# Long convolution and memory attention on one core: another stored order, other PSUM banks and other eviction engines for the same operations

## The chip, the cores and the metric

The kernel runs on one core of a Trainium2 chip. The core's engines work side by side, each on its own queue in order: TensorE (PE, with its weight loads shown apart as PEld), VectorE (DVE), ScalarE (ACT), GpSimd (POOL) and SyncE (SP), which here only issues DMAs. Matmul results land in PSUM, which has eight banks; DVE or ACT must copy a result out ("evict" it) before its bank can take another group of matmuls. The metric is device time in microseconds, as the median of several runs. A profile is one further execution, with a record of every instruction.

## The reference

Two branches, joined along the last axis. S = 2048 tokens, D = 640 channels.

```python
# branch A: short filter, gate, long convolution by FFT, skip, gate
k_shift = sum of 4 shifted copies of k, each times a tap per channel
kv = k_shift * v
y  = irfft(rfft(pad(kv)) * rfft(pad(ssm_k)))[:S]      # per channel
a  = q * (y + kv * ssm_D)

# branch B: 32 heads of 20, 4 segments of 512 tokens, one after another
q, k, v = x @ wq, x @ wk, x @ wv
p     = softmax(q @ k.T / sqrt(20) + causal mask)     # inside a segment
a_mem = (phi(q) @ M) / (phi(q) @ z + 1e-6)            # memory of earlier segments
o     = g * a_mem + (1 - g) * (p @ v)
M, z  = M + phi(k).T @ v, z + sum(phi(k))
b     = o @ wo
return concat([a, b], axis=-1)
```

## The kernel before

Nothing in this kernel is issued in the order in which its Python runs. A class `Recorder` takes down 1482 operations with their engines, and 471 PSUM groups. Then `Recorder.issue` (line 247) issues them in a stored order: `ORDER` (line 990) is a packed permutation of the operations, `BASE` (line 1012) a packed list with the first PSUM bank of each group. Dependencies are kept in any order: `issue` asserts that each operation comes after all that it depends on, and semaphores are placed from the final order. So the stored order sets, for each engine, the sequence of its queue; when an instruction runs follows from the queue and its waits. A third constant, `EVICT` (line 987), has one digit for each of 227 plain PSUM copies: `evict` (line 400) gives a copy to DVE where the digit is 1, to ACT where it is 0.

**Branch A** runs as `conv` (line 439) over five blocks `dp` of 128 channels. For each: the long filter is brought to time-major form in tile `kT` (`load_filter`; block 0 by four groups of PE transposes named `kt`, from a load named `sk` and the identity `ident`; blocks 1 to 4 by DMA transposes and a scratch tensor in DRAM), the short filter is applied by matmuls (`ks`, seven or ten to a group) on the transposed k (`kr`, load `lk`), and DVE multiplies each result by v (tile `vt`). `spectrum` (line 525) makes eight PSUM groups of DFT matmuls with the tables `Wf` (four loads, one per residue c), evicts each into tile `F` (128 x 512), and DVE combines them with six butterfly operations into `Kh` (filter; steps `BK`) or `Xh` (data; `BX`). `product` is 12 DVE operations and six more butterflies; `inverse` runs four groups of eight matmuls with the tables `Wi`, and DVE multiplies by q.

**Branch B** runs for eight units u: segment u // 2, head half u % 2. `project` (line 651) does, for each of four token tiles, two groups of five matmuls for k and q (evicted into `KQ`, 128 x 320) and one for v (evicted into `Va`), then a DMA transpose of KQ into `KQT` (queue SP). It also makes `phi`, a bound per query (`kam`, `bound`, small DMAs named `rows`) and the memory update (`mem`). `attend` (line 748) fills score groups with matmuls on 32 rows (`A` and `J` below the diagonal, `D` on it with its mask), ACT takes exponentials of 128 x 1024 from PSUM into a ring of seven tiles `ET`, and the value matmuls (`O`) read ET and Va; DVE normalises them into `o`. `project_out` (line 910) turns o and multiplies by `wo` (tile `outb`, groups `w`); the last segment is turned by PE (`ot`) and evicted through the spare tile `PP`.

At the start ten dummy matmuls on a zeroed tile (`warm`) occupy PE while the first loads are under way. x for the first segment is loaded in four parts (`xn`) and turned by PE (`xt`).

Of the kernel before, what the change touches and what calls it, by code (L numbers as in the profile page):

```python
# [21 lines left out]
S = 2048; D = 640  # L22
H = 32; DH = 20; NS = 4; L = 512
# [241 lines left out]
class Layer:  # L265
# [134 lines left out]
    def evict(self, out, in_, grp):  # L400
        e = self.evicts
        self.evicts += 1
        if EVICT[e] == "1":
            self.nc.vector.tensor_copy(out=out, in_=in_, grp=grp)
# [505 lines left out]
    def project_out(self, s):  # L910
# [41 lines left out]
        for t in range(4):  # L952
# [31 lines left out]
SKA = (0, 1, 2, 3, 4)  # L984
KQV, QN = 0, 4
TAP2 = (2, 3, 4)
EVICT = ("11000000110000001000000010000000000000000000000000000000000000100000000000001000010001001010100100100000000000000000110000000000000010000000"
         "000000000101000100100100000000000000000000001100001000000000000000000000010110010000011")
KQW, FW, WW = 1, 1, 1
ORDER = r"""  # L990
c-jTQ17H{c3<SVW@|kUSwr$&9XWO=I+qOCz?QGk&&ATkf3P(0%M-JpfB;*2+A7v2{xlszyP#Mut0p(B)QBfLIkOyf{0A)}JF%S!R5gFwXfH=s2il~Yx2!(toh~!!cDO3<2hCE8dL`}p-UhRT(S{Oy32t
+Mp)lA5yDK&#uM-6mCDy@S=NR8S^fb5zU^^jg0pc(3-FEXPm3Tu57(dGz^Bxr>;D5~*L0vWYCiXn%#Kr*yOBNWpn$fs?QTYI7*ifcc#L<#MU#^`~P+7wwd9onH6@@s1CgZAivuo#H6nnpXKKZ>H14n=Z
wMkmBYLKM;hIvAz3j1IzR3`0&Gf{{ptFc^Tb7=z&$g|a$LGwBo^hY=W$;uxm0wV;;MZJ4f^bvr8PaNU9OI#yGnfo8;JghMW!fT=nWlduz$F-OPg6g1S5n2xzxRV!*Eor+32Pj_Lwj?fvXrqy+VPQyqIL
JfVam9>`cM->g!QCd@HVmA(;jyBfC+C)cdZQYAmSg6gluI|AiZL0gQM4Raht*7;M4rb~>oJ0#fgxOfC9rP5E;w&cX7@e<M(NSBf+5&B*=P(zMq?4L0)6)pSJoME0I0M=d{L<dqS{Gos_ENXwXrn81A!c
be{jJfghc3cOU5fCw1t+iq6Lpn#*Q02w%P>i!$T4iv)w&!}EV{MVc6t~~5Y-~sAKk2Lw2uzZff`wY(OK7Oc=Xl3dL3PLF}i42izYX5AN_QY4%YMNua|HE>-8cw>Sb)u+X!b@Fhn2XD&kpeTc=TFHEv+2
-oj%%!Wuk599xMnwnv}h0m4aiiEOJ7L*m+c+`(RbhW#2-_UT>3w}W~Q8<4=(B9<kx1G-J0ql2wOfQjwUv)a*KAdbY6xUv!3^(D^fCM32XJ+E6ep2U_U_6l3HpLMdG+TS``YYQ*CHNLz-1RT*_n$%t+x&
2dEB1tUC?2xvxcQ~r2G%=3pTLj2yO<`yBum)=q3DM))My}}zeUFrOQa_-lwX_IwU2o`Rjc73}m0iOpw6fH4MI+fqT-D@qK|dp=rI3{J6)hw^5?Vy*ZeP&LE^2DKq@gU0+|;}J4QcF_-qZUU+HPwqNo$#
{xAm|e$ZARDjy}+T_>PB~#gfS{q?JCFK+;JzODK;tyZyya46t;T#|GMOw3Qr2NpE?ri)FBGme2mcCA|!>u9nd<*-#s1Z7qYev;5XkAbDkwWs(9`&_o7XU&|+jETiO>!lrV`ikL}G3nh7ExMh|Rmdmn8Q
E4YRrLYu~+?HQPS}_YPqbvoATQMmjB`lYWu?|wwidrEVYc;Kal(Ovd-2$z>WtGx4)5cjXt7h$Gmc6tbGTuJe536Cq>h{ViTXC6SVdSGJe_9u*VkKmv^^mGoN+#K4`(<UVla!RM(oK5G6dP@wrJPl;^7h
)EXm=?sQ>~1Il{fa!Dp?<yX8ok1^%Zcom6N&FU&`1gt8I1cv(>dZHr-}eDAu#r+EVJ<GY!oKw$K{cb8T#8rJ=piCf3vzSu=Z~i_O`PVc6W}SvZE}5Sec+?5%#Ym-^lo*gO4eN2NWNTX?o$BYv^+(t#1V  # L1000
!iGvq4v>|$#8z20S#1?$jXl+Y^3@`-lB~7gw#=5Aah<i2KUPs9GXl38d0Yb7jK^fXRhIhPU^{Jx?X~8tDh(Kgy(B94+ddm6(K$jkS~b~Zn{A|=kRXf3+T3DQq_=FfT{c{*%O3lxHRP=gk{EoiyX~DFww
SCf!PZ(rtS!H5U1`T7_Ct@_E3GBRY_J@+nml0Nv=$FqO^L;LJY;d$ij8@~x^s%mkU*&;+iaAaw9|IR&RQFuv(YkE;_`!bVQY?&_-w+d(vjn2lGI^rcI9}PCm(gDbmC-5!1LCWb$QAb$b9L>3)VyuahjZ
!gq$v?Bq@7vp`4eK(o~Z3qW#p)?8)9dCv&8pB;zcZE3>5!FGv6zNn$491Ubz5l7fpQCHt}-8%RGkmc!Ce`tvPQ@f}lhAk*;$(=a`k%1aJlT4vx9SuBH?k$L!@gLzRhF)#CRnLJ}=HkajcNt#I^e&BsRX
JJ0%1LkKDKH>@~z#GiUUR)_dn2p()gSS|amn~R|G7EF^CWrI1tdiR-&RiVEGctn3Sb{_Og{4`BWjT_$xmwEczFd{^tiV#dD{JH_OY)OGkZV$rW4Tt!_(b{2&w5YpSS40w6;|aqe&%?N;t_enb@GkXc*X
8oS-)kkIEJJ7gZFq@Ub8xH%LbXi8m#5F?TTENpPa;*EbQy$i%w*q&tehZD6<(Nb2ynd<c@5Yn=+MiS=4`V9&gDsPT?k*!H@jSivEe4Wjc3AG5^Eswu+VfhCP(kEahvsO&-Zs`Od$b&jnn_MO@6%{*PN^
E#X13j_X;&mvAY?E4%x0uHa5t$;WbsHT|uqKamZ5CQs!qzsoMUXH|S7H*vSTlV=vzpUYKyA@pV3BhT%nY~>HRX5rm@ue_4_{#wHMHtv(ntmkheh}*e?A7u+0_)fl;lKw$<v626j&+<t^`B(WR`=zmekp
uFWVf>r?mI%I^q5YvX@ja~TH|+`kNJM{Rk$f-raX%w_RDWVo`~VN~sa5x;p3?uxAvW{WUcvuLIgjS4yoKMlU`F?t{=#B;Y>(rj&=~%}%6l?T?#=y>#Pt;3(yMwrZ{-IijVJJgp2$txc!0<Ew4T^cQ}wZ
>^J<>n&+sIVFo|dMOrF6{F@#5%#oKvS&*s@Zhf~k8hiCSr-r9S)>oMl^T;A4u`enBF;|#5N`~<Hsly>yIp3fV4ZqM%>yptFAa}1*eyt8-l^9-k5J*-|}3Ge0wy|#zfI^Nr(X?MTKe%{~v_$3bTfj-Im`
c+2IK|a|F`CuR8Q+&0L^N2dshxu?H;n%pv$9q&A;$uCEuJkxM!K3R)ALXljhDX-KI?-qQb;i|MKF8<!XrJeiG>K02`99MZ_*!4*F*K%5^JE%NW9f8X=!-moF7_q9)R*~kkFD!{g>UdZ9$%B{5l^UleWP
#oM7qfXG|2b)Q9tGfeT(n+t$xUl`(Z!e+kJ<h@L=EOJ3YjA`ELIYeKp$N  # L1010
"""
BASE = r"""
c-mc30g?nD2qH86|Bo*b+ufU{GBZNd04x~%&bTx0ns;wsVABs;$<=x9*NVF?t;Ty0?OflYUD3Gb!~1n-SztuovFZ0a%3nVn{+bWf7}IF|!Wq-Cbp|81egJP%FUlJ9#&+Ewa@gcwoXgX1piGB#NSVe1Z7
0j|`_r$^hloyAF7=j}SF{nubYqGhY`pU!(^71UT~`EBq%wiD=vp+R*`dGMHyr10V|G)~t!(p)1DFq#c|1h>mj{$>l4UaQMP1|7!ijx2k_=};DARxb^!(-D85-4S<oHp`pO&L-aEJU;E2C;o9?dM(N%2P
eL%ljRj%R<czI6%p)#R4aCDcowH>04x9xzou9#VIJQ7uy^I{pB12L?C
"""


# [69 lines left out]
```

## Time and profile before

| | before |
|---|---|
| median of 3 runs (lowest, highest) | 271.61 us (271.2, 271.77) |
| span of the profiled execution | 271.3 us |
| granted TensorE clock, mean | 1.000 |
| weight loads (PEld), busy | 194.0 us (71%) |
| POOL, busy | 7.2 us (3%) |

The page gives busy time by engine, then groups of instructions, then the chain of work that ended last. An ACT or DVE instruction's recorded time overlaps the next one's by a little: the step from one start to the next start is what a queue really pays for an instruction, and is read from a timeline; the mean of a group is somewhat larger. Matmul ends are modelled, so for PE too the starts are what counts.

### The profile page before, as it was taken

Reading aid. Unit: us, or ns where it says so; the run is one execution under the profiler, and the core shown is the slowest. Engines: PE = TensorE matmul, PEld = TensorE weight load, DVE = VectorE, ACT = ScalarE, POOL = GpSimd, SP = SyncE. Lnnn points to the kernel's source line nnn. Section 1 sums busy time; section 2 is a strip of 40 time slices with the busy share of each in tenths; the row PEclk is TensorE's granted clock in tenths of the full one; section 3 lists DMA queues with packets and bytes.
Section 4 is the critical chain, followed back from the end, with each engine's and each line's share of the span. In section 5 each row is a group of like instructions: output and inputs, shape, how many; then the busy total and the mean of one; then the engine's idle time right before and its main releaser. Section 6 shows DMA issues by size and latency. Waiting matters only on the chain.

```text
span 271.3 us, 10053 instructions
## 1 busy us (share of the span) xinstructions
PE 259.8 (96%) x4335; PEld 194.0 (71%) x4335; DVE 246.4 (91%) x385; ACT 249.7 (92%) x394; POOL 7.2 (3%) x18
## 2 busy tenths in 40 slices
PE   6999999999999999999999999999999999988994
PEld 2688768877767677877767788778776776565772
DVE  0268999999999999999999999999999999999972
ACT  2676899999899999999999999999999999999952
POOL 8200000000000000000000000000000000000000
PEclk9999999999999999999999999999999999999999
DMA  6997989999999869997997679996970094635124
GB/s 196 274 217 143 235 178 208 190 243 258 211 164 262 189 153 169 156 183 153 172 219 156 180 148 216 162 170 123 201 165 17 30 159 99 154 89 126 47 51 126
DMA packets 131516, 44.72 MB, mean 165 GB/s; under 512 B 121899, under 2 KB 129072, under 8 KB 131344
## 3 DMA queue, kind: packets, MB, share of 16 engines
q1 hardware_dynamic: 131328, 43.96, 80.0%
q8 instruction: 34, 0.56, 0.9%
q0 software_dynamic: 144, 0.12, 0.2%
q14 instruction: 10, 0.08, 0.1%
HBM read 14.05 MB, written 7.34 MB: 79 GB/s over the span
## 4 chain that ended last, share of the span: by engine, by line
PE 66%; ACT 18%; DMA 8%; SPq 3%; issue 2%; DVE 2%; ACTq 0%; DVEq 0%
PE ps L256 66%; ACT ET L256 12%; DMA Wi<-c_wi 3%; SPq L256 3%; ACT F L256 2%; DMA Y<-in_B_x_dram 2%; DMA KQT<-qabs 1%; ACT Va L256 1%; DMA pq<-in_A_q_dram 1%; ACT outb L256 1%; ACT KQ L256 1%; DVE PP L256 1%; ACT PP L256 1%; DVE o L256 0%; DVE outb L256 0%
## 5 line engine op out<-in xcount | busy, mean ns | idle before, releaser
L256 ACT ACTIVATE ET<-ps 128x1024 bf16<-128x1024 f32 x160 | 162.4, 1113 | 0.4 <-PE ps L256 0.4
L256 PE MATMUL ps<-wqkv,xT 128*128 128x320 bf16 x480 | 78.2, 302 | 0.6 <-ACT ET L256 0.3
L256 PEld LDWEIGHTS <-xT 128*128 128x128 bf16 x640 | 58.0, 98 | 28.8 <-issue 7.1
L256 ACT CAST F<-ps 128x512 bf16<-128x512 f32 x72 | 43.9, 683 | 1.3 <-PE ps L256 1.3
L256 PE MATMUL ps<-Va,ET 128*128 128x21 bf16 x1280 | 41.9, 173 | 0.0
L256 PEld LDWEIGHTS <-ET 128*128 128x128 bf16 x1280 | 39.3, 96 | 3.3 <-issue 2.1
L256 PE MATMUL ps<-KQT 32*128 32x128 bf16 (+2 forms) x896 | 34.8, 239 | 0.6 <-DMA KQT<-qabs 0.4
L256 PEld LDWEIGHTS <-Wf 128*128 128x128 bf16 x320 | 29.6, 98 | 6.5 <-issue 1.6
L256 ACT CAST KQ<-ps 128x320 bf16<-128x320 f32 x56 | 26.7, 522 | 1.8 <-PE ps L256 1.8
L256 PE MATMUL ps<-wo,xT 128*128 128x320 bf16 (+2 forms) x160 | 25.5, 299 | 1.3 <-ACT ET L256 1.3
L256 PEld LDWEIGHTS <-KQT 32*128 32x128 bf16 x896 | 16.5, 92 | 10.1 <-issue 7.6
L256 PE MATMUL ps<-kT,Wf 128*128 128x256 bf16 x160 | 22.2, 273 | 0.0
L256 PE MATMUL ps<-vt,Wf 128*128 128x256 bf16 x160 | 21.6, 273 | 0.2
L256 PE MATMUL ps<-Y,Wi 128*128 128x256 bf16 x160 | 20.8, 273 | 0.8 <-DMA Wi<-c_wi 0.8
L256 DVE TENSOR_TENSOR o<-ps,rr 128x640 bf16<-128x640 f32 x24 | 19.7, 820 | 0.4
L256 PE MATMUL ps<-Mbd,PqT 128*128 128x84 bf16 x96 | 18.3, 202 | 1.1 <-ACT ET L256 1.0
L256 DVE TENSOR_TENSOR Y<-Y,pq 128x2048 bf16<-128x2048 bf16 (+1 forms) x20 | 18.6, 943 | 0.0
L256 DVE TENSOR_TENSOR pq<-Xh,Kh 128x2048 bf16<-128x2048 bf16 x15 | 18.3, 1219 | 0.0
L256 ACT CAST Va<-ps 128x320 bf16<-128x320 f32 x31 | 16.0, 536 | 2.2 <-PE ps L256 2.2
L256 PEld LDWEIGHTS <-Wi 128*128 128x128 bf16 x160 | 14.7, 98 | 3.5 <-DMA Wi<-c_wi 1.0
L256 PE MATMUL ps<-skd,kr 128*128 128x128 bf16 (+4 forms) x116 | 16.7, 257 | 0.0
L256 PEld LDWEIGHTS <-kr 128*128 128x128 bf16 x116 | 14.8, 149 | 2.3 <-issue 1.0
(86 smaller groups left out, 363.2 us busy)
## 6 DMA issues: line engine op xcount, KB each, us to landing
vt<-in_A_v_dram SPq DMA_DIRECT2D x10, 256.0 KB
pq<-in_A_q_dram SPq DMA_DIRECT2D x10, 256.0 KB
turned<-kT SPq DMA_DIRECT2D x4, 512.0 KB
kT<-turned SPq DMA_DIRECT2D x8, 256.0 KB
out_dram<-pq SPq DMA_DIRECT2D x8, 256.0 KB
out_dram<-outb SPq DMA_DIRECT2D x12, 160.0 KB
kb<-kr SPq DMA_DIRECT2D x6, 256.0 KB
Wf<-c_wf SPq DMA_DIRECT2D x4, 256.0 KB
```

What stands on the lines that cost most here:

```text
L256: f(*[fix(a) for a in args], **{k: fix(v) for k, v in kw.items()})
```

## The change

The operations, their operands and the tiles are the same. Three constants change: `EVICT`, `ORDER` and `BASE`.

```diff
-EVICT = ("11000000110000001000000010000000000000000000000000000000000000100000000000001000010001001010100100100000000000000000110000000000000010000000"
-         "000000000101000100100100000000000000000000001100001000000000000000000000010110010000011")
+EVICT = ("11001001110010010010000000000100000000000000000000000000000000000101000000010000011000000010000000110000000110000000000000000100000010000000"
+         "001000000001111100000000000000010000000010000001100001001001000000110001000000010110101")
 KQW, FW, WW = 1, 1, 1
 ORDER = r"""
-c-jTQ17H{c3<SVW@|kUSwr$&9XWO=I+qOCz?QGk&&ATkf3P(0%M-JpfB;*2+A7v2{xlszyP#Mut0p(B)QBfLIkOyf{0A)}JF%S!R5gFwXfH=s2il~Yx2!(toh~!!cDO3<2hCE8dL`}p-UhRT(S{Oy32t
...
+c-jTQ17H{c3<SVW@|kUSwr$&9XWO=I+qOCz?QGk&&ATkfifqV^9LR}W$cWsi1|SjwQ3`bs5jBw?(NG;kZ3xmJIts#27<rHywNM&0P!|Qz1`SXKt<V~g(E^o`0c8;z4N(q-pooQ*D37*?gQ!T0_{fB$$ctvEf~ts#
...
```

Unpacked, this is what differs.

**Evictions.** 32 of the 227 copies stood on DVE, and 43 stand there now: 31 go from ACT to DVE and 20 from DVE to ACT. Net, DVE gets two more copies of F, two of KQ, five of Va, one of 128 x 640 (xT), and one each of kT, xT and PP with 128 x 512, and gives up one of qabs (128 x 512) and one of outb (128 x 320): 11 in all.

**Order.** On PE 416 of the 510 recorded operations (a group of matmuls, or part of one) stand at another place of the queue, by 5.4 places on average and 40 at most. The number of places at which an operation on 32 rows follows one of another kind falls from 82 to 78. On DVE 351 operations are displaced, on ACT 352, on SP 159 of 180.

**The start** differs most. The first entries of three queues:

```
SP before : w(k) ident xn.1 xn.0 xn.3 xn.2 sk w(q) Wf.0 Wf.2 Wf.3 lk Wf.1 lv lv w(v) ...
SP after  : sk ident xn.0 Wf.3 Wf.0 Wf.2 xn.3 xn.1 Wf.1 w(q) xn.2 w(k) lk lv lv ...

PE before : warm x6, beta, warm, taps, xt.1 xt.0 xt.3, warm x2, xt.2, warm, P0, P3, kt.1, P1, kt.2,
            P2, P0, P1, kt.0, kt.3, P2, FK x3, ks.3, FK x2, ks.0, FK x3, P3, ks.1, ks.2, kx, V0, FX ...
PE after  : warm x7, kt.2 kt.3 kt.1, beta, taps, kt.0, warm, xt.0, FK x4, xt.1, warm, FK, xt.3,
            FK x3, P0, xt.2, P1, P3, P1, P2, P0, ks.3 ks.2 ks.1 ks.0, P3, P2, FX x8 with kx ...

DVE before: memset, taps, xT, beta, KQ, beta, KQ x3, kT, F, phi x2, beta, kam, F, kam, ks.3, kam,
            ks.0, BK, ks.1, ks.2, BK x3, kx, BK x2 ...
DVE after : memset, kT, taps, beta, kT, xT, F, beta, xT, F, F, BK x3, KQ x2, BK x2, ks.3, BK, beta,
            ks.2, ks.1, ks.0, KQ, phi x2, kam ...
```

Here P0 to P3 are k and q projections by token tile, FK and FX the DFT groups of filter and data. In the order before, the projections of the first unit come first and the filter's DFT after them; now the filter's transposes and its whole DFT come first. The end of the queues is alike in both: the last PE group is the projection of token tile 1, its copy is ACT's, and its store is SP's last DMA.

**Banks.** 406 of the 471 groups have another first bank.

More of the change, by code (lines that the diff above doesn't have):

```diff
@@ L989 @@
 KQW, FW, WW = 1, 1, 1
 ORDER = r"""
[L991 to L1010, printed above, removed]
+c-jTQ17H{c3<SVW@|kUSwr$&9XWO=I+qOCz?QGk&&ATkfifqV^9LR}W$cWsi1|SjwQ3`bs5jBw?(NG;kZ3xmJIts#27<rHywNM&0P!|Qz1`SXKt<V~g(E^o`0c8;z4N(q-pooQ*D37*?gQ!T0_{fB$$ctvEf~ts#
@@ new lines @@
+=4gT_sE1?-g{EkP3aF39Xor*<4;_&X6_G&`!jVTipeTwU22yEWZI5(X30buml4}>lMJHs`zUYng+7sQ7P5U7^x}q}z&>dN{1oCMgWY=EkffPCtg*B~)Mt&`%MRYidYB3#+96AaEF%-ph1QMe^24M__p@a^`0F=~H
+Iu-@AwC2_!$fV<t8O2c&sgMX^kq_fhMpJ77q|wYe0Xem-Cc#`Sr;`u{({v)Xp`Z@a$(XIVw1SS+;o3l_V2<uUd7Y=@bUUW&6s@EcwUO?}RLnqCovM{}8V+EwHq>yau6t2U7itaNiA6dcHFY1V=q~I=pw`lvn5cU&
+Umt62t)nA!GZyGc)YXwXMo*!>hG3G;&?P!vPvZz?>IAK)(QFnv=o~cGGia`}(L$T(EN!YSbuQ*32+cG-T4{9aq?2{2cGP)TfumTa2hm!Op{H)aa&4n4bSn;_m;TY?=&cLzSHoL34QmS#!B*-CjM7Euu08ZHMr#xc
+XKi(rZqi6{7OQnJ!Xv5$qn)nN_PSPSopm`j>N-7#uKG*WmS7p~;x;zudhMbEbSe6%*=CI*1GTTZ_0#_PTO&(!8Ki^tJTBoeF5oHR*>&8(J%q7~xQy5~MDODYo?tbeVW>X9Rm8Elb`xuG1Mw}Yh$XOSvPbu7B3qA#
@@ new lines @@
+*r$<gB_3e|ZebMyEV1p^gSt&)*a6+H&k@sJVu!xKTCBrajVJLXmc7DxeT`6dPUA>i3DQ`yRXbS>i7i_+v~{+f`UWwjr@g~&?O;i4mnOB1=xB)~Ku+mtO)W_!ft=AzNG6B$h$gqg8mzr6nZ3nPeUD=rq6y`=rm!@U
+(yr-sy@qgdLQiT-Yh`UDwMDcWdReb%c<E<XwY8<P5BR5TY=HH*Pxy$>NMn&~pj}W{N=axD<)WsNwDJX+?UH7(#1cX7>Q{Wj58TwOc295VZA~us^^T^Hw(>x~Bb)t2I{Al(nnWJyPvo#c*4+l%Z?w1UmdAS7ALO;R
+*3R--I?G^v?HAHZM(b?_C6jfr^w!ndNgvA~`6Z`ilC*ZoavKGb-!e*O$z=tsy%e-8l2e9SAsc2z#YLo$<dVWx%nC>mD{e(?xRtPOR!mA-DJyLwtfplZmE1DYI!Y}w8De>5l!cNpHr4_ypH#D%Hp}uz4;g3GEwt3I
+o|0Y0TL(#r95TTwTNUdj|E#K&u}M}~o@fyPUt4#1X=Uw=y|Qdl-ik{(n`pua7;T;8la-XoR>72?ZHj%c?^a4GS|$5o(`~B#v=Z{sI!hNREn%gM)V5z%PG;CN>ne3DjD+TFt81ZH&%W7vd#eMazRj^l*4XA+0}I0@
@@ new lines @@
+*3jN*QwzstHc(#cLJP|``q!FUSy^n)^ou>$Ve-}HSqm#KFLaR&m+*|p1y(^CvZB1y`fNn!avLJ^ZI!i<6?Rl2akWL}8XGDrZLPIn6t-kbsU&UrRM%MpuD2zY0__-;H5rY4WU2kOT8z$Dy396OW%*+<7?V|HgjAD}
+vdP}-2HR|XWxEC07CSCmZHHBnoz_nVNg(&yTZ_g1Qk#RNy7ZFv+-Ei9o%NPoX6(TIw#QmYYl*-(B%ATOHfJ3Pl#^0hYDrBQC1d5VebC(&Vn6hV1=~?OX2<QTe$;Pzz~XV69kLTPMNV2=&XO^5+74QGPLor1#?D$}
+#^y0OXQO4ROqX#oL%J|N&)Ym1FEizWb!8LIm%7r5r)0LY<^-w31nkIetjk24Bnu=Vn@Cb#v=h>ao!NsuIa%t-Lg~%J?8CmCBgxp0^`)t_;aN$}{+ufTJTFN&fDI%u&&dT@Bq>;rjU*Kt$|p_9rIMQIn4XPgv1DLI
+X5wc}!zJ>TO_`Z#nT7B9j?3i(2XdL@VROmLi*lc*<&0dCLCnWOe89nc#=?Bghb+PuTq*hah*_D9+4+*qWQ7!9LFV99`KdX1O>*%Ti}D6@^Rlgy+bqsIc9W~61dH*mt(6fR$;;A<6QvaIN=Xjk6&cGlQkrFWPu59U
@@ new lines @@
+4&``WmvX!>S8N;)%MBUMO8m_7tjsEWAXQm`6*-Kf_=T_dmDO0CuUXW;=skYp7*615-jo_%gFiTlPq{&ES+Lx;V*ZA;{GQF^PuBE_{LWi4i<3E<fgU33We%rsDu1zz&t+LJ?9(`pzgfhu+ilq{^SM!G@P<w2AMTJ<
+tmvC%lWdVST+NSsD39b5EBOL0<ThEv#azq3yd%$SJ^yj5tm9P+lFAOhX3tH0377J*EN2zJ!<}-ME4hJ3WUs8?Mm~{U@=QwkGQO65vWe#Or=niZ!+JP>BfI6MeU#GfzDL6QCwVTL`9i)*eg7$+rGf|Xmo)IV@<q0C
+8@F&f-$`}f!SC{3zR3>><@@E8e2|j9lP@KV@8V-N^2UBZB6w(T;t@TPKjCif;a>ihecaE;-qfS|0UqQbKCxyV#Z&rI`zNV9wMX;1{zqE)LyPGzES5+2M;6=T_+N?Z$vlQP_xl#l<9iBE?o~aFKd@>Z%tHbdP3NX9
+J%K0ma-PToJgv9#gHqnp`)OwI#}>lGp2Rcy8LB4rlWgsoJgZYrv5g;LHqY*^IXtIl_M^<@Jv@uI^PYZ;q4X?!d2v6^++M=lduZ+GVKk5D^%KnJ`Mr~O@Gf4!JNso8^ea5aa9YUEv#VcVH^0b+9$v39toHWqevN&+
@@ L1011 @@
+w%75tzS8@7e~+L8e3cLMNq(J!e6SDkh}zeq>ST|uV?3G;^<h56$N6xNq9c5)kM}q_(MS3OALWsBhOhOwnpkK1OpmN{e4Wqrc|OZW`+T43@id7}^JE%dW9R~3=+ixc#?;lm$P;R8UF=JIsjv4-OsZ@Ah;Q~~zQLD!
+kO$}r-{`S)lPA)He$)^7VL#@_J=pj77T@b3e!{o<KHuj1{eW-x9lq0d`ELIYb9~y~
 """
 BASE = r"""
-c-mc30g?nD2qH86|Bo*b+ufU{GBZNd04x~%&bTx0ns;wsVABs;$<=x9*NVF?t;Ty0?OflYUD3Gb!~1n-SztuovFZ0a%3nVn{+bWf7}IF|!Wq-Cbp|81egJP%FUlJ9#&+Ewa@gcwoXgX1piGB#NSVe1Z7
-0j|`_r$^hloyAF7=j}SF{nubYqGhY`pU!(^71UT~`EBq%wiD=vp+R*`dGMHyr10V|G)~t!(p)1DFq#c|1h>mj{$>l4UaQMP1|7!ijx2k_=};DARxb^!(-D85-4S<oHp`pO&L-aEJU;E2C;o9?dM(N%2P
@@ L1015 @@
-eL%ljRj%R<czI6%p)#R4aCDcowH>04x9xzou9#VIJQ7uy^I{pB12L?C
+c-lph0TRR@2m=vO|NrBYP3qODRSQWB%*cpXcl1*+V#m4PbHD4(<E|&W$$H<YLq?zG9i5qXw>Y1?9j(>4BUv@Z@Sh2Kkyqq4;{pE=-^d3RVfLJ0G|NV7#|OOn1~`pcoQQRT6`Th91FN(raSKHo#z1qSYmk+Xv15v?
+?U=zkyy|}g*OaNd6iVjvN1pxBmhqQs@!kF~H&#3sIx@LOS(ENnII6pR8vEa;a#=@scg!F!%Bpp;@k1&nINN@e8PhtpS(1!N+(CinO@$9x6YN0`BpTEYWd<Rw=Yv=`^(ecb47srEkh*8Mit=d_^}Q3N@myc-=RikV
+kLs<84fn93^SPe({Bu2gDp$69akzKYq04&G?r$>XUODf>pT6^8Ocbc1i<<ucP%j1<
 """
```

## The prediction

> **What bounds the kernel now.** I read the page first, then busy time by stretches, then the waits, then the starts of single instructions on the queues.
>
> ```profile
> span 271.3 us, 10053 instructions
> PE 259.8 (96%) x4335; PEld 194.0 (71%) x4335; DVE 246.4 (91%) x385; ACT 249.7 (92%) x394; POOL 7.2 (3%) x18
> GB/s 196 274 217 143 235 178 208 190 243 258 211 164 262 189 153 169 156 183 153 172 219 156 180 148 216 162 170 123 201 165 17 30 159 99 154 89 126 47 51 126
> PE 66%; ACT 18%; DMA 8%; SPq 3%; issue 2%; DVE 2%; ACTq 0%; DVEq 0%
> ```
>
> The chain of work gives PE 66% and DVE 2%, which looks like a PE kernel. The table by stretches says otherwise (columns: length, then PE, PEld, DVE, ACT and POOL busy, each with its count, clock, DMA share, GB/s):
>
> ```profile
> 0.00:12.00 12.00, 9.54 (x51) 5.04 (x52) 1.44 (x4) 5.12 (x11) 7.21 (x18) 1.00 0.90 249
> 12.00:24.00 12.00, 11.98 (x104) 9.89 (x103) 8.01 (x17) 9.56 (x24) 0.00 (x0) 1.00 0.78 170
> 24.00:60.00 36.00, 35.52 (x500) 26.86 (x499) 35.65 (x50) 32.41 (x61) 0.00 (x0) 1.00 1.04 208
> 60.00:100.00 40.00, 38.70 (x685) 29.48 (x682) 39.01 (x54) 39.29 (x62) 0.00 (x0) 1.00 0.94 205
> 100.00:150.00 50.00, 49.45 (x858) 37.66 (x856) 49.19 (x81) 50.00 (x77) 0.00 (x0) 1.00 1.01 175
> 150.00:200.00 50.00, 49.98 (x908) 38.04 (x908) 49.51 (x80) 49.99 (x78) 0.00 (x0) 1.00 0.87 169
> 200.00:218.00 18.00, 17.93 (x334) 13.37 (x323) 17.90 (x30) 18.00 (x27) 0.00 (x0) 1.00 0.26 56
> 218.00:254.00 36.00, 33.24 (x707) 23.86 (x706) 35.76 (x58) 36.00 (x49) 0.00 (x0) 1.00 0.60 126
> 254.00:271.30 17.30, 13.48 (x217) 9.79 (x216) 9.97 (x19) 9.30 (x13) 0.00 (x0) 1.00 0.27 71
> ```
>
> From 24 to 254 us three engines are full at once. DVE's idle time there is 0.35 + 0.99 + 0.81 + 0.49 + 0.10 + 0.24 = 2.98 us; PE's is 0.48 + 1.30 + 0.55 + 0.02 + 0.07 + 2.76 = 5.18 us, half of it in 218 to 254, where ACT has none. DVE has room only ahead of 24 us (9.45 of 24 used) and behind 254. So work that is added to DVE is paid in full, unless it is done before 24 us. The chain hides this: it names the engine that was last at each step, and where all are full that is mostly PE.
>
> **The change, part by part.** *Evictions.* Steps between starts on the two queues (timelines; start, time, engine, instruction):
>
> ```profile
> 15.32 0.89 DVE L256 CAST KQ<-ps 128x320 bf16<-128x320 f32 x2 [0.26 <-PE ps L256]
> 17.79 0.69 DVE L256 CAST F<-ps 128x512 bf16<-128x512 f32 x1 [0.60 <-ACT skd L256]
> 18.39 0.48 DVE L256 TENSOR_SCALAR qabs<-KQ 128x1280 bf16<-128x1280 bf16 x1
> 8.00 0.82 DVE L256 CAST xT<-ps 128x640 bf16<-128x640 f32 x1 [1.72 <-PE ps L256]
> 8.74 0.17 DVE L256 TENSOR_SCALAR rr<-A 128x32 f32<-128x32 f32 x1
> 95.49 0.86 ACT L256 CAST F<-ps 128x512 bf16<-128x512 f32 x1
> 95.96 0.73 ACT L256 CAST Va<-ps 128x320 bf16<-128x320 f32 x1
> 96.27 0.90 ACT L256 CAST F<-ps 128x512 bf16<-128x512 f32 x1
> ```
>
> On DVE a copy of 512 columns takes 18.39 - 17.79 = 0.60, one of 640 takes 0.74, and one of 320 takes 0.40 (two in 0.89, less the 0.49 of the second). On ACT 512 columns take 0.47 and 320 take 0.31; 640 scaled from these is about 0.6. Net, DVE gets four copies of 512 (two F, kT, xT and PP, less one qabs), one of 640 and six of 320 (two KQ, five Va, less one outb): 4 x 0.60 + 0.74 + 6 x 0.40 = 5.54 us more on DVE, and 4 x 0.47 + 0.6 + 6 x 0.31 = 4.3 us less on ACT.
>
> The rows from 100 us on show ACT at 50.00, 49.99, 18.00 and 36.00 of as much, DVE at 98 to 99%. The Trainium skill (Perfetto Trace Analysis, Identifying the Most-Contended Engine) says to optimise the engine with the highest occupancy, and not to judge TensorE by matmul busy time. By it ACT at 92% comes first and its 4.3 us would come off the span; by the rows the 5.5 us on DVE have to be set against that. The trace bears the rule out only for 218 to 254 us, where PE idles and ACT does not.
>
> *The start, PE.* Starts on PE before:
>
> ```profile
> 1.26 2.74 PE L256 MATMUL ps<-o 128*128 128x512 bf16 x6 [1.26 <-DVE o L256]
> 4.59 0.18 PE L256 MATMUL ps<-outb,ident 1*128 1x32 bf16 x1 [0.60 <-DMA outb<-in_B_beta_dram]
> 5.43 0.62 PE L256 MATMUL ps<-ident,qabs 5*64 5x5 bf16 x12
> 7.25 1.04 PE L256 MATMUL ps<-ident,Y 128*128 128x128 bf16 x8 [0.36 <-DMA Y<-in_B_x_dram]
> 10.10 2.58 PE L256 MATMUL ps<-wqkv,xT 128*128 128x320 bf16 x10
> 12.52 0.41 PE L256 MATMUL ps<-ident,kT 128*128 128x128 bf16 x4
> 13.70 2.26 PE L256 MATMUL ps<-wqkv,xT 128*128 128x320 bf16 x15
> 15.80 0.66 PE L256 MATMUL ps<-ident,kT 128*128 128x128 bf16 x8
> 21.20 1.52 PE L256 MATMUL ps<-kT,Wf 128*128 128x256 bf16 x12
> 22.56 0.84 PE L256 MATMUL ps<-wqkv,xT 128*128 128x320 bf16 x5
> ```
>
> Three projection groups take 15.80 - 13.70 = 2.10 (0.70 each), four matmuls of `kt` 0.66 - 0.41 = 0.25, three DFT groups 1.36 (0.45 each), a group of x some 0.55 (eight matmuls in 1.04, with about 0.16 of tail), a warm group 0.43 (six in 2.74, with the same tail). Six of these from 1.26 on end at 3.84, and beta starts at 4.59: 0.75 lost; x costs 0.36; the two projections at 10.10 took 2.42 for 1.40: 1.0. Together 2.1. After: seven warm groups at 0.43 run to 4.3. sk and ident (544 KB) come first on SP, and the first slice moved 196 GB/s over 6.8 us, latency included: 0.56 MB by about 2.9, say 4.3 with the latency unspread. Three kt to 5.1; taps waits for its load as now (5.43) to 6.2; kt, warm and xt to 7.4; four DFT groups to 9.2; xt, warm, DFT, xt to 11.2; three more DFT groups to 12.6. Data: everything through Wf.2 is 1.51 MB, there at 7.4 us by 196 GB/s for 6.8 us and 274 after it; through w(q) 2.51 MB, at 11.1. Each comes before its use, by 0.5 us at the least. From 12.6 the projections run with their data there, ks from 17.3 to 20.8. Against the 2.1 us lost before, 0.4 are lost here (0.3 at taps): PE is **1.7 us ahead**. If the first loads land as late as x does now, nothing is left of that (0); if nothing waits, 2.1.
>
> *The start, DVE.* Before 24 us DVE did 9.45 us of work. After, with the steps above: two kT, two xT, three F and four small ones, 4.9 us, by 13.3. Then the butterflies of the filter, which need all eight groups:
>
> ```profile
> 23.61 1.23 DVE L256 TENSOR_TENSOR Kh<-F 128x2048 bf16<-128x2048 bf16 x1 [0.68 <-ACT F L256]
> 25.95 1.22 DVE L256 TENSOR_TENSOR F<-F 128x2048 bf16<-128x2048 bf16 x1
> 27.09 1.29 DVE L256 TENSOR_TENSOR Kh<-Kh 128x1024 bf16<-128x1024 bf16 x2
> ```
>
> Two at 27.09 - 25.95 = 1.14 and four at 0.60 (two in 1.29, less 0.08 of tail) are 4.7; with three KQ (1.2), four products of ks (2.4, by the 0.60) and 0.5 of small ones: it is 13.7 by 24. The last of these wait for PE, so it isn't more. DVE gains 13.7 - 9.45 = **4.3 us ahead of 24**, and pays 5.5: the end by DVE's account moves by +1.2 with every later gap kept, and by 1.2 - 2.98 = -1.8 if all its idle time from 24 to 254 closes.
>
> *Order after the start.* A group of projections takes 243.69 to 244.36 = 0.67 before one like it, and 231.31 to 232.09 = 0.78 before scores on 32 rows:
>
> ```profile
> 231.31 0.85 PE L256 MATMUL ps<-wqkv,xT 128*128 128x320 bf16 x5
> 232.09 0.53 PE L256 MATMUL ps<-KQT 32*128 32x256 bf16 x8
> 243.69 0.84 PE L256 MATMUL ps<-wqkv,xT 128*128 128x320 bf16 x5 [0.29 <-ACT ET L256]
> 244.36 0.84 PE L256 MATMUL ps<-wo,xT 128*128 128x320 bf16 x5
> ```
>
> Four such changes fewer (82 to 78) at 0.11 save 0.4 us. Waits that go or come with the order and the banks are what I can't price from rows. The longest that PE has now:
>
> ```profile
> PE ps L256 <- ACT ET L256: 3.4, 10, 0.5
> PE ps L256 <- DMA Wi<-c_wi: 0.8, 1, 0.8
> ```
>
> The load of Wi stands at place 41 of SP's queue, before at 43 and behind two copies for block 2: its 0.8 may go, and what is then late is DVE's work of the same stretch. The bounds for all of it: PE loses its 5.18 us of idle time (a gain of 5.2), or loses as much again. I take nothing for PE, and for DVE that 2.6 of its 2.98 us close, since each of its gaps waits for PE or ACT, PE being 1.7 ahead and ACT 4.3 lighter. SP carries the same 180 DMAs; a DMA that is late through its place in SP's queue shows as a wait of PE or DVE and lies in these bounds. Behind the last PE operation nothing changes: the same copy on ACT and the same store.
>
> *The sum.* By PE: 271.3 - 1.7 - 0.4 = 269.2. By DVE: 271.3 + 1.2 - 2.6 = 269.9. The later one decides: **269.9 us of span**. The median (271.61) is 0.3 above the span of the profiled execution, so I forecast **270.2 us**.
>
> **The rivals.**
>
> 1. *ACT was the bound, and its relief comes through.* For it: ACT without idle time from 100 to 254, PE's ten waits for ET. Against: DVE is as full, and only 218 to 254 shows PE idle beside a full ACT. 271.3 - 4.3 = 267.0, so 267.3 as a median. By the Trainium skill's rule above this is the case to expect. Chance 0.20.
> 2. *DVE takes back what it was given.* The head start of 4.3 and the 5.5 of copies stand against each other, and only 1.3 of the gaps close: 271.3 + 1.2 - 1.3 = 271.2, as a median 271.5, which can't be told from before. For it: 98 to 99% on DVE in each stretch. Against: ACT's relief. Chance 0.23.
> 3. *The head start fails, and the kernel is slower.* The butterflies stand in DVE's queue ahead of two KQ copies and all products of ks, and need the last table. Wf.1 is the ninth load, 2.1 MB with what is ahead of it: 9.5 us by the rates above, 10.7 at 196 GB/s throughout. From a landing behind 11.2 (where PE comes to it) each us late is a us for everything behind it on DVE, and PE stops as banks aren't copied out. At 13.2, the 2 us take 2 of the 4.3: 271.3 + 1.2 + 2.0 - 1.0 = 273.5, as a median 273.8. Chance 0.20.
>
> That the change isn't made as told is excluded: the two unpacked orders are permutations of the same 1482 operations.
>
> **How the numbers follow.** The forecast has 0.37, with its own range from 269.2 (2.98 closed and PE's account reached) to 271.0. Faster by over 0.2% (about what a measurement of this kernel can tell from no change; under 271.07): 0.37 + 0.20 = 0.57; within it 0.23; slower 0.20. The range runs from 267.2, the ACT case, to 272.8, which is DVE's account with all gaps kept (271.3 + 1.2 + 0.3); beyond it lie most of rival 3 and the lower edge of rival 1.
>
> **What would show it.** The count of `F` copies on DVE goes from 8 to 10, of `KQ` from 8 to 10, of `Va` from 1 to 6. The first `Kh` butterfly should start near 13.3 us (23.61 before), and DVE should have some 13.7 us busy before 24. In 24 to 254 DVE should have under 1 us idle and ACT for the first time several; ACT full and DVE idle there would speak for rival 1, a first `Kh` behind 15 us for rival 3. The first projection should start at 12.6. I am wrong in the base if PE's idle time from 24 to 218 grows by more than 2 us: then the new order makes waits that no row of before could show.

## The result and the profile after

The changed kernel takes **279.85 us** (median of 4 runs, 279.32 to 281.07) against 271.69 us for the kernel before in the same comparison (4 runs, 271.2 to 272.08): ratio 1.0317, interval 1.0272 to 1.0362. It is slower by 8.2 us where 270.2 was forecast, and lies above the upper edge of the range, 272.8. The time is about 1.8 us more than the span in each run of both kernels that gave the two; the profiled execution of after has a span of 277.7 us (time 279.5). Before's profiled span of 271.3 is one of its longer ones (in a later comparison a run of 271.66 us had 269.8), so the two traces differ by 6.4 us, the medians by 8.2.

The page of after, span, busy time and chain:

```profile
span 277.7 us, 10064 instructions
PE 259.7 (94%) x4330; PEld 192.7 (69%) x4335; DVE 256.4 (92%) x396; ACT 248.8 (90%) x383; POOL 7.2 (3%) x18
DVE 7%; PE 6%; issue 2%; ACT 0%; DVEq 0%
```

DVE has 11 instructions more and 10.0 us more busy time, though the copies were worth 5.5. The chain can be followed back over 15% of the span only; it is no help here. Busy time by stretches (columns as before):

```profile
0.00:12.00 12.00, 9.69 (x75) 6.31 (x77) 3.64 (x9) 5.44 (x11) 7.15 (x18) 1.00 0.83 250
12.00:24.00 12.00, 11.83 (x96) 9.22 (x95) 11.26 (x19) 8.74 (x26) 0.00 (x0) 1.00 0.91 184
24.00:60.00 36.00, 34.83 (x490) 25.35 (x490) 34.57 (x51) 32.93 (x59) 0.00 (x0) 1.00 1.10 188
60.00:100.00 40.00, 37.96 (x687) 29.01 (x685) 39.41 (x54) 39.18 (x60) 0.00 (x0) 1.00 0.98 195
100.00:150.00 50.00, 48.37 (x814) 36.17 (x813) 49.38 (x78) 48.85 (x77) 0.00 (x0) 1.00 0.95 181
150.00:200.00 50.00, 48.58 (x873) 36.36 (x871) 48.71 (x79) 47.97 (x71) 0.00 (x0) 1.00 0.99 162
200.00:218.00 18.00, 17.85 (x309) 12.82 (x305) 17.86 (x30) 17.81 (x26) 0.00 (x0) 1.00 0.61 123
218.00:254.00 36.00, 32.98 (x704) 24.62 (x705) 35.53 (x59) 35.40 (x49) 0.00 (x0) 1.00 0.57 102
254.00:277.70 23.70, 17.65 (x307) 12.79 (x304) 16.02 (x27) 12.45 (x15) 0.00 (x0) 0.93 0.33 81
```

The start is good: DVE does 3.64 + 11.26 = 14.9 us before 24, against 9.45. Four starts on PE and one on DVE there:

```profile
8.21 2.12 PE L256 MATMUL ps<-kT,Wf 128*128 128x256 bf16 x16 [0.82 <-DVE kT L256]
13.10 0.84 PE L256 MATMUL ps<-wqkv,xT 128*128 128x320 bf16 x5
17.92 3.49 PE L256 MATMUL ps<-skd,kr 128*128 128x384 bf16 x27
21.25 0.98 PE L256 MATMUL ps<-wqkv,xT 128*128 128x320 bf16 x6
...
14.46 1.22 DVE L256 TENSOR_TENSOR Kh<-F 128x2048 bf16<-128x2048 bf16 x1 [0.57 <-ACT F L256]
```

Projections begin at 13.10, the short filter (ks) at 17.92, the butterflies at 14.46. But what was gained is spent by the end: behind 254 us DVE has 16.0 us of work left, against 10.0 before. From 24 to 254 DVE is still busy for 98%, ACT has room now, and PE's idle time from 24 to 218 is 1.17 + 2.04 + 1.63 + 1.42 + 0.15 = 6.4 us, against 2.4. PE's waits say for whom (engine, tile, what it waited for: us in total, times, longest); the first six rows of after, then the one row of before in which PE waits for DVE:

```profile
PE ps L256 <- DVE o L256: 4.6, 11, 1.3
PE ps L256 <- ACT ET L256: 2.6, 6, 1.4
PE ps L256 <- DVE pq L256: 1.2, 2, 0.8
PE ps L256 <- DVE qabs L256: 0.9, 3, 0.4
PE ps L256 <- DVE Y L256: 0.9, 1, 0.9
PE ps L256 <- DVE kT L256: 0.8, 1, 0.8
```

```profile
PE ps L256 <- DVE o L256: 1.3, 1, 1.3
```

Both rows of `o` contain the 1.26 us at the very start in which PE waits for the zeroed tile, which bears this name. Without it PE never waits for `o` before, and ten times, 3.3 us in all, after. So DVE is behind. Its timeline shows why. After, near the end (start, time, instruction):

```profile
239.01 0.35 DVE L256 RECIPROCAL rr<-ps 128x32 f32<-128x32 f32 x1
239.40 0.82 DVE L256 TENSOR_TENSOR o<-ps,rr 128x640 bf16<-128x640 f32 x1
240.14 1.22 DVE L256 TENSOR_TENSOR pq<-Xh,Kh 128x2048 bf16<-128x2048 bf16 x1
...
252.55 1.22 DVE L256 TENSOR_TENSOR Y<-Y,pq 128x2048 bf16<-128x2048 bf16 x1
253.80 1.23 DVE L256 TENSOR_TENSOR Xh<-Y 128x2048 bf16<-128x2048 bf16 x1
254.94 0.35 DVE L256 RECIPROCAL rr<-ps 128x32 f32<-128x32 f32 x1
255.33 0.82 DVE L256 TENSOR_TENSOR o<-ps,rr 128x640 bf16<-128x640 f32 x1
256.19 0.33 DVE L256 TENSOR_TENSOR o_s<-o 128x320 bf16<-128x320 bf16 x1
```

The same instructions in the trace of before:

```profile
162.32 0.36 DVE L256 RECIPROCAL rr<-ps 128x32 f32<-128x32 f32 x1
162.59 0.27 DVE L256 TENSOR_TENSOR o_s<-o 128x320 bf16<-128x320 bf16 x1
162.77 0.82 DVE L256 TENSOR_TENSOR PP<-PP,qabs 128x1280 bf16<-128x1280 bf16 x1
163.50 0.82 DVE L256 TENSOR_TENSOR o<-ps,rr 128x640 bf16<-128x640 f32 x1
...
239.71 0.35 DVE L256 RECIPROCAL rr<-ps 128x32 f32<-128x32 f32 x1
240.10 0.82 DVE L256 TENSOR_TENSOR o<-ps,rr 128x640 bf16<-128x640 f32 x1
```

A reciprocal takes 162.59 - 162.32 = 0.27 of the queue if the next instruction is about something else, and 240.10 - 239.71 = 0.39 if the next is the product that reads it. After shows the same for other forms: the product `o` takes 0.74 (239.40 to 240.14) or, with the sum of its halves right behind, 0.86 (255.33 to 256.19); 128 x 2048 takes 1.14 (253.80 to 254.94) or 1.25 (252.55 to 253.80). Whatever the form, an instruction that depends on the one right ahead of it in DVE's queue starts **0.12 us later**. I call such a pair dependent neighbours. The later one of them reads what the one ahead writes (67 of the pairs after) or overwrites what it uses (19). Counted in the stored orders, **before has 26 of them and after 86**. Sixty more by 0.12 is 7.2 us.

The recorded busy time hides this. A reciprocal is recorded with 0.35; where the next starts at 0.27 they overlap by 0.08, where it starts at 0.39 there is a gap of 0.04. Two thirds of the loss look like more busy time, the rest like gaps too small to be put down to anything.

To sum it, I took for each form the step to the next start where the next does not depend (lower quartile), and added up what each step from 24 to 254 us has beyond it:

| excess of DVE's steps, 24 to 254 us | at dependent neighbours | at all other places |
|---|---|---|
| before | 2.98 us (22 pairs) | 3.19 us |
| after | 9.08 us (74 pairs) | 2.24 us |

A second thing shows at the end. Windows of 2 us of after (the number behind the engines is the granted clock):

```profile
254.00:256.00 2.00, 0.59 (x16) 0.22 (x12) 1.97 (x3) 2.00 (x3) 0.00 (x0) 1.00 0.27 62
256.00:258.00 2.00, 1.90 (x84) 1.84 (x76) 1.93 (x4) 2.00 (x3) 0.00 (x0) 1.00 1.00 208
258.00:260.00 2.00, 1.12 (x15) 0.72 (x6) 1.97 (x4) 2.00 (x3) 0.00 (x0) 0.72 0.00 0
260.00:262.00 2.00, 2.00 (x39) 1.27 (x38) 1.68 (x4) 0.25 (x2) 0.00 (x0) 0.50 0.00 0
262.00:264.00 2.00, 2.00 (x44) 1.91 (x43) 1.23 (x3) 1.92 (x2) 0.00 (x0) 0.92 0.17 39
```

Behind PE's waits from 254 on, the clock is at half for some 3.4 us (1.1 + 2.0 + 0.3), in which PE does 1.7 us less than at full clock.

### The profile page after: what moved, and what is told of

It is laid out like the page before. It is cut to its first block, busy times and chain, and to the rows that moved or that the text cites. A ratio compares the mean times of both kernels' runs of the same rounds, so it can differ in the third digit from the quotient of the medians.

```text
span 277.7 us, 10064 instructions
## 1 busy us (share of the span) xinstructions
PE 259.7 (94%) x4330; PEld 192.7 (69%) x4335; DVE 256.4 (92%) x396; ACT 248.8 (90%) x383; POOL 7.2 (3%) x18
## 5 line engine op out<-in xcount | busy, mean ns | idle before, releaser
L256 ACT ACTIVATE ET<-ps 128x1024 bf16<-128x1024 f32 x160 | 159.9, 1070 | 6.8 <-PE ps L256 5.5
L256 PE MATMUL ps<-wqkv,xT 128*128 128x320 bf16 x480 | 75.9, 299 | 0.5 <-DVE vt L256 0.2
L256 ACT CAST F<-ps 128x512 bf16<-128x512 f32 x70 | 41.2, 642 | 2.9 <-PE ps L256 2.8
L256 PE MATMUL ps<-Va,ET 128*128 128x21 bf16 x1280 | 40.7, 173 | 0.2 <-ACT ET L256 0.2
L256 PEld LDWEIGHTS <-ET 128*128 128x128 bf16 x1280 | 38.3, 96 | 1.7 <-issue 1.0
L256 PE MATMUL ps<-KQT 32*128 32x128 bf16 (+2 forms) x896 | 33.3, 241 | 3.7 <-DVE o L256 2.0
L256 ACT CAST KQ<-ps 128x320 bf16<-128x320 f32 x54 | 23.2, 469 | 4.6 <-PE ps L256 3.4
L256 PE MATMUL ps<-vt,Wf 128*128 128x256 bf16 x160 | 22.3, 272 | 0.4 <-DVE outb L256 0.2
L256 PE MATMUL ps<-pack 32*128 32x128 bf16 x512 | 14.9, 219 | 3.1 <-DVE pq L256 1.2
L256 PEld LDWEIGHTS <-pack 32*128 32x128 bf16 x512 | 8.7, 93 | 10.6 <-issue 10.3
```

The costliest lines, as they stand in the source:

```text
L256: f(*[fix(a) for a in args], **{k: fix(v) for k, v in kw.items()})
```

## The experiments

Theory N: the time was lost at the dependent neighbours. Rival C: the 11 copies make DVE too full whatever the order. Rival O: the order on PE, the banks and the DMAs cost the time, or copies that do not fit them. In the order experiments only DVE's queue is permuted; the queues of PE, ACT and SP, the banks and the operations stay. Diffs of an order show DVE's queue unpacked, each operation by its step and the tile that it writes (P1 to P3 and YB are steps of `product`, I of `inverse`, N the normalisation). All ratios are to the kernel before on the same chip.

| run | neighbours | us | ratio (interval) |
|---|---|---|---|
| e1: after, pulled apart | 14 | 284.42 | 1.0465 (1.0401 to 1.0530) |
| e2: after, old `EVICT` | 89 | 291.01 | 1.0717 (1.0643 to 1.0791) |
| e3: before, pushed together | 86 | 276.05 | 1.0150 (1.0093 to 1.0207) |
| e4: before, pulled apart | 12 | 276.73 | 1.0172 (1.0107 to 1.0237) |
| e5: before, new `EVICT` | 31 | 296.85 | 1.0953 (1.0890 to 1.1016) |
| e6: after, dependencies cut | 55 | 276.16 | 1.0184 (1.0108 to 1.0260) |
| e7: before, the same cut | 14 | 272.26 | 1.0012 (0.9979 to 1.0045) |
| e8: after, pulled apart with care | 39 | 275.69 | 1.0164 (1.0088 to 1.0239) |
| e9: before, pulled apart with care | 24 | 272.09 | 1.0018 (0.9989 to 1.0046) |
| e10: e8 with the cut of e6 | 25 | 273.46 | 1.0068 (1.0042 to 1.0094) |

**e3: before, with as many neighbours as after.** 53 of DVE's operations were moved by a few places, from 26 neighbours to 86.

```diff
 BX Xh
-BX Xh
 beta Mbd
+BX Xh
 P1 pq
-BX Xh
 ks vt
+BX Xh
 P1 Y
```

> The kernel before, with DVE operations moved by up to four places so that 86 instead of 26 neighbours in DVE's queue depend on each other, as many as in the changed kernel; copies, banks and the other queues as before. Theory N: 60 x 0.12 = 7.2 us more at most, 277 to 279 us. Rivals C and O: no change, 271.5 to 272.5.

Measured: 276.05, 4.6 us slower than the 271.46 of before in that batch, and a little below the 277 that theory N had as its lower edge. The excess at neighbours from 24 to 254 us rose from 2.98 to 9.4, elsewhere it fell from 3.19 to 0.82. The granted clock was 1.0 in all four runs, so this is without any loss of clock. Busy time of the page of e3:

```profile
PE 260.4 (95%) x4333; PEld 194.0 (71%) x4335; DVE 251.0 (91%) x385; ACT 252.3 (92%) x394; POOL 7.2 (3%) x18
```

With the same 385 instructions DVE's busy time grows from 246.4 to 251.0: the overlap that the neighbours lose. Sixty neighbours cost 4.6 of the 7.2 us that the bare product gives; by the two sums, part of them falls where DVE would have waited.

**e1 and e4: pulled apart crudely.** In after (86 to 14, 62 operations moved) and before (26 to 12, 14 moved), DVE operations were shifted by up to four places wherever a pair stood, with the dependencies kept and nothing else asked. From e1:

```diff
 F copy
-beta rr
 xT copy
 F copy
 F copy
-BK Kh
-BK Kh
+beta rr
 BK Kh
 KQ copy
+BK Kh
+BK Kh
 KQ copy
```

> The changed kernel, with single DVE operations moved by a few places so that 14 instead of 86 neighbours in DVE's queue depend on each other; the copies, the banks and the other queues' contents are the same. Theory N (a DVE instruction that needs the one right ahead of it starts about 0.12 us later, and DVE is full): 72 x 0.12 = 8.6 us less at most, so 271 to 273 us. Rival C (the eleven more copies on DVE cost the time): no change, 279 to 280. Rival O (the order on PE, the banks and the DMAs cost it): no change, 279 to 280.

> The kernel before with 12 instead of 26 dependent neighbours on DVE. Theory N: 14 x 0.12 = 1.7 us less at most, 270.0 to 271.2 us. Rivals C and O: no change, 271.5 to 272.

Measured: 284.42 and 276.73, 4.6 us slower than after and 5.3 slower than before. Theory N in its plain form missed both. The neighbours' excess did fall, to 1.29 us in e1 and 1.49 in e4, but at other places it rose to 15.6 and 8.85. The waits of e1, for PE's and for DVE's largest:

```profile
PE ps L256 <- DVE o L256: 8.3, 10, 1.3
DVE rr L256 <- PE ps L256: 7.1, 10, 1.3
```

In after these stand at 4.6 and 1.5. A reciprocal that is brought forward stands in the queue before its matmuls are done, and all of DVE waits with it; a product that is put back frees its bank later, and PE waits. A move for 0.12 us costs up to 1.3. That these two kinds of move are the cause is read from the waits; e8 tests it.

**e8: pulled apart with care.** From after again, but an operation is moved only if what it reads had been ready in after's trace with a margin at the new place, and none that reads PSUM is put back. 39 moved, 86 neighbours become 39.

```diff
 BK Kh
-BK Kh
-BK Kh
 KQ copy
+BK Kh
+BK Kh
 KQ copy
 BK F
-BK Kh
 ks vt
+BK Kh
```

> The changed kernel with DVE operations moved by up to four places, and only where the trace shows that the moved one has its data by then, that no instruction that frees a PSUM bank comes later, and that no other engine comes to wait: 39 instead of 86 dependent neighbours. Theory N: 47 x 0.12 = 5.6 us less at most, 274.5 to 277 us. If the gain is again eaten by waits as in the cruder separation: 280 or more. Rival O: no change, 279 to 281.

Measured: 275.69, as theory N had it: 47 fewer neighbours, 4.2 us less than after, with all 43 copies still on DVE. The excess at neighbours is 4.25 us (34 pairs), elsewhere 4.55. The two waits now, from the same view of e8 (the 1.3 of the first row is again the one at the start):

```profile
PE ps L256 <- DVE o L256: 2.8, 5, 1.3
DVE rr L256 <- PE ps L256: 1.9, 3, 1.3
```

**e6 and e7: the dependency cut, the order left.** `o` takes a constant tile in place of the reciprocals, and the sum over the halves of `o` reads a table. 31 of after's 86 neighbours no longer depend; in before, the control, 12 of 26 (the expectation has 11).

```diff
             num = pov[:, :, :, 1:DH + 1]
+            rr = self.taps.rearrange("p n c -> p (n c)")[:, 0:16 * nb].rearrange("p (b x) -> p b x", x=16)
...
-in0=o2[:, 0].rearrange("p (q h) e -> p q h e", h=4), in1=o2[:, 1].rearrange("p (q h) e -> p q h e", h=4)
+in0=self.Wf[:, 0, 0, 0:320].rearrange("p (q h e) -> p q h e", q=4, h=4), in1=self.Wf[:, 0, 1, 0:320].rearrange("p (q h e) -> p q h e", q=4, h=4)
```

> The changed kernel, every queue in the same order, but the normalisation no longer reads what the instruction ahead of it makes: the product reads a constant tile in place of the reciprocal, and the sum of the two halves reads a table in place of the product (so the attention's output is not normalised and not summed). The instructions, their shapes and their number stay; 31 of the 86 dependent neighbours on DVE go, none of DVE's other waits. Theory N (0.12 us per dependent neighbour on a full DVE): 31 x 0.12 = 3.7 us less at most, 276 to 278 us. Rival O (the order on PE, banks and DMAs): no change, 279 to 281.

> The kernel before with the same two operands replaced as in the run on the changed kernel. Here 11 of the 26 dependent neighbours on DVE go. Theory N: 11 x 0.12 = 1.3 us less at most, 270.2 to 271.4 us. If the cut itself speeds the kernel up by another way, this control gains as much as the run on the changed kernel.

Measured: 276.16, which is 3.7 us less than after, while the control stays at 272.26 and gains nothing. So the operations have not just become cheaper. But the 1.3 us that theory N allowed as a gain in the control did not come either: the interval leaves room for 0.6 at most. The neighbours' excess fell there from 2.98 to 1.9 us, and elsewhere it rose by some 0.5. In e6 it fell by 2.6, from 9.08 to 6.5. Besides, 21 of its products stand behind a reciprocal that they no longer read and take 0.06 less themselves (last section), 1.3 us together. So that the 3.7 us agree with 31 x 0.12 is in part luck. The timeline of e6, at the place that was shown of after:

```profile
236.90 0.35 DVE L256 RECIPROCAL rr<-ps 128x32 f32<-128x32 f32 x1
237.17 0.76 DVE L256 TENSOR_TENSOR o<-ps,taps 128x640 bf16<-128x640 f32 x1
237.85 1.21 DVE L256 TENSOR_TENSOR pq<-Xh,Kh 128x2048 bf16<-128x2048 bf16 x1
```

Same queue, same neighbours, one operand changed: the step behind the reciprocal is 0.27 and no longer 0.39. This is the closest to a measurement of the disputed price by itself.

**e10 and e9: both together, and before with care.** e10 has the order of e8 and the cut of e6; 25 dependent neighbours stay, one fewer than in before. e9 applies the careful moves to before, where only two are to be found:

```diff
 I pq
+phi PP
 N o_s
-phi PP
...
-YB Xh
 N rr
 N o_s
+YB Xh
 N o
```

> The order of e8 (39 dependent neighbours on DVE) with the cut of e6: o reads a constant tile in place of its reciprocal and the sum over halves reads a table, so branch B's output is neither normalised nor summed. 14 of the 39 dependencies go, 25 stay, one fewer than before has. Theory N (what the new order lost over before is the 0.12 us at each dependent neighbour): 14 x 0.12 = 1.7 us come off the 275.7 of e8, 274.0, range 273.2 to 274.8, and a remainder of some 2.5 us over before stays, which is not the neighbours'. Rival (with 39 left the neighbours no longer decide, as in the cut of before, where 11 went and nothing came of it): 275.2 to 276.2.

> The kernel before with one or two DVE operations moved by a place or two, so that 24 dependent neighbours stay of 26; nothing else changed. Theory N and its rivals agree: 2 x 0.12 = 0.24 us at the most, 271.2 to 271.9, not to be told from before. It asks whether the order before can be bettered by this rule at all.

Measured: e10 273.46, 2.2 us less than e8 (1.7 expected; the intervals of the two just overlap) and 6.4 less than after; it is 0.7% above before. e9 272.09, not to be told from before: at 26 neighbours such moves have nothing left to win. No version tried beats the kernel before.

**e2 and e5: evictions and order exchanged.** After with before's `EVICT`, and before with after's:

```diff
-EVICT = ("11001001110010010010000000000100000000000000000000000000000000000101000000010000011000000010000000110000000110000000000000000100000010000000"
+EVICT = ("11000000110000001000000010000000000000000000000000000000000000100000000000001000010001001010100100100000000000000000110000000000000010000000"
```

> The changed kernel with the EVICT of before: its order and banks, eleven copies fewer on DVE; 89 dependent neighbours on DVE. Theory N: DVE has 5.5 us less of copies but 3 x 0.12 more of neighbours, so 274 to 276 us if DVE is the bound, and still slower than before by some 3 us. Rival C: 271 to 273, all of it back. Rival O: 278 to 280, or more, as the order was made for other copies.

> The kernel before with the new EVICT: its order and banks, eleven more copies on DVE, 31 dependent neighbours. If a fuller DVE is what costs: 5.5 us of copies and 0.6 of neighbours, 276 to 278 us. If the order must fit the copies, as the changed order with the old EVICT suggests (291 us), it is well above that, 280 to 290. If ACT's relief counts, under 271.

Measured: 291.01 and 296.85, both far above either kernel; e2 is 15 us above what theory N had, and e5 above all that was expected. So copies and order belong together. These runs exchange all 51 copies that differ, so they do not show what the 11 more on DVE cost by themselves. That they are not the main cause is shown by e3, which is slow without them, and by e8 and e10, which win back most of the time with them. The waits of e5:

```profile
ACT F L256 <- PE ps L256: 10.0, 8, 2.5
PE ps L256 <- DVE F L256: 5.1, 3, 2.9
DVE Xh L256 <- ACT F L256: 5.0, 1, 5.0
```

A copy that changes its engine takes its old place in another queue: there it is too early, and all behind it wait for its matmuls, or too late, and its bank is missing. That is read from the waits. For or against theory N these two runs show nothing, because such waits cover it.

## Why the prediction was wrong

The step that failed is DVE's account behind the start: the prediction closed 2.6 us of DVE's idle time and put nothing on DVE for the order itself. In its place the runs show 60 more dependent neighbours, which add 6.1 us to DVE's steps from 24 to 254 us. Step by step, as the prediction put it:

- **Evictions, +5.54 us on DVE:** right in kind and number (F 10, KQ 10, Va 6 copies on DVE), but not all of what DVE got.
- **The start, PE 1.7 us ahead:** nearly. The first projection starts at 13.10 (forecast 12.6) and the matmuls of ks end by 21.25 (20.8), since PE waits 0.82 us for DVE's `kT`, which was put at nothing. It is some 1.2 us ahead.
- **The start, DVE 4.3 us ahead:** the term was too small; 14.9 - 9.45 = 5.4 us were gained. The first butterfly started at 14.46 and not 13.3, of which 0.57 is a wait for a copy of ACT. Rival 3, which needed a late table behind 15 us, did not come.
- **"For DVE that 2.6 of its 2.98 us close, since each of its gaps waits for PE or ACT":** this failed. The sentence counts only gaps between recorded times. DVE's recorded idle time from 24 to 254 is 4.54 us (1.43 + 0.59 + 0.62 + 1.29 + 0.14 + 0.47), and behind the recorded busy time the steps themselves had become longer.
- **"Waits that go or come with the order and the banks are what I can't price from rows":** they were bounded by 5.2 us for PE and then taken as nothing, while PE's waits for DVE's `o` grew from none to 3.3 us behind the start. For the largest loss the rows were there. Before's trace has 18 reciprocals of 0.27 and 10 of 0.39, and the diff's order, unpacked, gives the count of 26 and 86. The order was compared by how far operations move, not by which ones become neighbours.
- **Wrong in the base if PE's idle time from 24 to 218 grows by more than 2 us:** it grew by 4.0.
- **Rival 1:** ACT got its room and the time did not follow. The rule of the Trainium skill quoted in the prediction (Perfetto Trace Analysis, Identifying the Most-Contended Engine), by which ACT came first, did not tell the outcome here: the relief of the engine with the highest share was paid for on an engine as full. As the order changed with it, the run is no test of the rule by itself.
- **Rival 2** (DVE takes back what it was given) had the right engine, but as an account of copies alone, 271.2.
- **From span to median, +0.3:** this sets the median of several runs beside the span of one execution. Where a run has both, the time is 1.8 us above the span, and the profiled execution of before was a long one.

DVE's account, with the missing term: 271.3 + 5.5 of copies - 5.4 of head start + (9.08 - 2.98) at neighbours - (3.19 - 2.24) elsewhere = 276.5 us of span; measured 277.7. It covers 5.2 of the 6.4 us between the two traces. The stretch at half clock is 1.7 us of PE at the most, in the right place for the 1.2 that is left.

What the runs show of the 8.2 us between the medians: sixty neighbours alone cost the kernel before 4.6 (e3), with 47 fewer after loses 4.2 (e8), and with 61 gone (e10) 6.4 are gone, some 0.8 of which is the second gain behind 13 reciprocals. The last 1.8 were not taken apart. The clock is the candidate: after's four runs had a mean granted clock of 0.979 to 0.994, e10's 0.985 to 0.994, while e3 with 1.0 was slowed by neighbours alone. One stretch of 3.4 us at half makes 0.994. The seven runs of e10 at 0.994 have a median of 272.8 us, its four at 0.985 to 0.988 one of 274.6, which fits the clock but does not single it out. A run that fills PE's waits behind 254 us was not made, so how much of it is the clock, and how much the copies, stays open.

## What to carry to other kernels

Before judging a new order on a full in-order engine, count the instructions that depend on the one right ahead of them, and take the price from two rows of one form, one with such a neighbour and one without; busy shares and idle times hide it. Pull such pairs apart only with operations that are ready and that free nothing another engine waits for: 0.12 us is won at a place, and up to 1.3 lost. Evictions that were chosen for one order do not carry over to another: here exchanging them alone cost 11 us (e2) and 25 us (e5).

## What the runs showed of the hardware

The price was the same for every form that occurs at least three times in after's trace: 0.11 to 0.12 us for instructions whose step is 0.27 to 1.14 us (21 reciprocals from 0.268 to 0.385 as median, 10 products `o` from 0.741 to 0.858, 14 butterflies and sums of 128 x 1024 from 0.602 to 0.719), except three of five `phi` steps, with 0.18. It makes no difference whether the later instruction reads or only overwrites: 10 of the 14 only overwrite, and so do four of 128 x 1280 that go from 0.733 to 0.856. The Trainium skill (VectorE: DVE Perf Modes, The DRAIN you can't avoid) has a test in which a semaphore behind each of eight copies "costs nothing extra here". Carried over to dependent neighbours, that would make sixty more of them free; the skill does not say there whether these copies depended on each other. Here e6, with one operand changed, and e3 show the price, and the measurement decides.

An independent instruction right behind a reciprocal also takes 0.05 to 0.06 less than elsewhere: `o` takes 0.68 in e6 (237.17 to 237.85) and 0.74 in after (239.40 to 240.14), and the 17 such instructions in the trace of before, of six forms, all show it. So a reciprocal and its reader pulled apart can win 0.18.

The granted clock goes to 0.50 for a stretch of 3.4 us although PE was busy for 1.90 of the 2 us from 256 to 258. What sets it off was not tried.
